# Lightweight convolution and MetaFormer block: the second group's x and tap products moved ahead, the third group's y stored by another queue

## The chip, the cores and the metric

The kernel runs on one core of a Trainium2 chip. The core has five engines that run side by side, each through its own queue in order: TensorE (PE in the profile, its weight loads PEld), VectorE (DVE), ScalarE (ACT), GpSimd (POOL) and SyncE (SP, which here only issues DMAs). The metric is the device time of one execution in microseconds (us); smaller is better. All data are float32.

## The reference

`x` has shape (8, 4224, 192), batch by sequence by channels. The first half is a causal depthwise convolution: 8 heads of 24 channels, 7 taps for each head, softmax over the taps. The second half is a layer norm without bias, two matrix products with a relu between them, and a residual:

```python
w = softmax(weight)                                   # 8 heads x 7 taps
y[b, s, h, :] = sum_k w[h, k] * x_padded[b, s + k, h, :]
xn = (y - mean(y)) / sqrt(var(y) + 1e-6) * g_ln
out = y + maximum(xn @ w_ch1, 0.0) @ w_ch2            # 192 -> 768 -> 192
```

## The kernel before, in words

**Groups.** The 8 x 4224 rows are laid on 128 partitions and cut into groups numbered from 0. Group 0 has 6 rows for each partition, group 1 the 8 rows for each partition that are left over at the ends of the batches, every later group 16 (the last one 10). In what follows x1, y1 and so on are the x and y of group 1; "the second group's x" is x1, "the third group's y" is y2, "the fifth x" is x4. y0 and y1 share one tile (rows 0 to 5 and 6 to 13), as do their later forms.

**The steps for one group.** `load_x` brings x with six rows of overlap. `first_tap` has ScalarE write y = tap 0 times x, head by head; `conv` has VectorE add the other taps into y, one instruction for each tap and head (L415). From group 2 on `second_tap` has ScalarE write the second tap's product into a tile of its own (`tb`), which four accumulating DMAs, issued by GpSimd in `add_in_parts` (L407), add into y; group 2's product lies in `room` and is added by VectorE (L1056). `transpose` turns y into blocks of 32 for TensorE (`yt`), `moments` takes the statistics, `root` has GpSimd compute the inverse deviation. TensorE multiplies by w1 (L521) and by w2 (L793, or L846); `store_y` writes y to the output, and the scaled result of the second product is later added there by accumulating DMAs (L942).

**Order.** The order is written out by hand: each engine does its instructions in the order in which the code issues them, and waits for the others by semaphores. Groups 0 and 1 go through plain products (`up`, `down`); from group 2 on `up_mixed` and `down_fast` make seven products instead of eight out of sums of quarters (`sums_of_quarters`, `sums_of_y`, on VectorE and GpSimd). Part of their sums are added by accumulating DMAs from GpSimd's queue (`close` with a part, L599, tiles `parts_cs` and `parts_tb`), part by VectorE straight from the accumulator banks (L641). Relus in place are ScalarE's L648.

**The banks.** The eight accumulator banks are taken in turn, singly (`take_bank`) or by four (`take_set`). A product that takes a set waits until ScalarE or VectorE has emptied it: in `up`, block f waits for the eviction (L511) of block f - 2, or for the copies of w1 if these took the set.

**The beginning.** The weights come as 64-bit words. `split_words`, `join_low`, `join_sign` and `join_product` make floats of them on VectorE and ScalarE; w1 in three parts s (x0 is on its way meanwhile), w2 after group 0's convolution. A load with `gate=True` is held until VectorE has written one element of its tile. `centre_w1` has TensorE take the mean out of w1 and do three of group 0's heads by `conv_on_pe`; `copies_of_w1` spreads w1 over four blocks of 32 partitions by TensorE, and ScalarE copies them out (L358). The third of these calls stands in `up`, behind block 1 of group 0.

**SyncE's queue** in this stretch: w1's words, x0, w2's words (L988, into `raw`), x1 (L140), y0's store, x2, y1's store, x3, x4 (L149, when x2's buffer is free), y3's store. y2's store (L487) is issued by GpSimd, inside `up_mixed(2)`.

Of the kernel before, what the change touches and what calls it, by code (L numbers as in the profile page):

```python
# [16 lines left out]
def kernel(  # L17
# [29 lines left out]
    nc = tc.nc  # L47
    PSUM = bass.MemoryType.PSUM
    B, S, D = x.shape
    H, K = weight.shape  # L50
# [41 lines left out]
    def rows_of_out(g, j1, j2):  # L92

        b, j0, n = groups[g]
        if b is not None:
            return [(slice(0, P), outr[b, :, (j0 + j1) * D : (j0 + j2) * D])]
        left = out[:, P * R : S].rearrange("b (p r) d -> p b (r d)", p=LP)
        return [(slice(0, P), left[:, :, j1 * D : j2 * D])]
# [17 lines left out]
    def take_bank():  # L116
        i = turn[0] % 8
        turn[0] = i + 1
        return all_banks[:, i]
# [126 lines left out]
    def join_low(raw, mant, power):  # L246
        mant = mant.bitcast(F32)
        nc.vector.scalar_tensor_tensor(
            out=mant, in0=raw[:, :, 0], scalar=2.0**-52, in1=mant, op0=ALU.mult, op1=ALU.add
        )  # L250
# [64 lines left out]
    def tap_matrices(h, ks=range(K)):  # L315
        for k in ks:
            nc.scalar.mul(diag[:, h - PE_HEADS[0], k, :], unit, taps[:, h, k : k + 1])

    def conv_on_pe(h):
        n = groups[0][2]  # L320
        cs = slice(h * GRP, h * GRP + GRP)
        pc = take_bank()[:, 0 : n * GRP]
        for k in range(K):
            nc.tensor.matmul(  # L324
                pc, diag[:, h - PE_HEADS[0], k, :], xg[0][:, k : k + n, cs],
                start=(k == 0), stop=(k == K - 1),
            )
        nc.scalar.copy(y[0][:, 0:n, cs], pc.rearrange("p (j d) -> p j d", d=GRP))

    def centre_w1():  # L330
        pm = [take_bank()[:, 0:FH] for r in range(2)]
        for r in range(2):
            nc.tensor.matmul(pm[r], share[0], w1f[:, r, :], start=True, stop=False)
        conv_on_pe(PE_HEADS[2])
        for r in range(2):
            nc.tensor.matmul(pm[r], share[1 + r], w1f[:, 2, :], start=False, stop=True)
        tap_matrices(PE_HEADS[1], range(3))
        for r in range(2):
            nc.scalar.copy(mean[:, FH * r : FH * r + FH], pm[r])
        tap_matrices(PE_HEADS[1], range(3, K))  # L340
        conv_on_pe(PE_HEADS[0])
        copies_of_w1(0, [(q, 0) for q in range(NQ)])
        conv_on_pe(PE_HEADS[1])
        copies_of_w1(2, [(NQ, 0), (NQ + 1, 0), (NQ, 1), (NQ + 1, 1)])

    def copies_of_w1(s, parts):
        pw = [take_bank() for q in range(NQ)]
        for q in range(NQ):
            rows = slice(C * q, C * q + C)
            nc.tensor.matmul(pw[q][:, 0:FH], copy[rows], w1f[rows, s, :], start=True, stop=False)  # L350
        for q, (c, r) in enumerate(parts):
            rows = slice(C * q, C * q + C)
            nc.tensor.matmul(
                pw[q][:, 0:FH], less[rows], mean[rows, FH * r : FH * r + FH],
                start=False, stop=True,
            )
        for q, (c, r) in enumerate(parts):
            nc.scalar.copy(w1[:, c, FH * r : FH * r + FH], pw[q][:, 0:FH])  # L358
# [8 lines left out]
    def first_tap(g, heads=(0, H)):  # L367
        n = groups[g][2]
        if g == 1:

            y[g] = y[0][:, groups[0][2] :]
        elif heads[0] == 0:
            y[g] = ypool.tile([P, J, D], F32, tag="y", name=f"y{g}")
        for h in range(*heads):
            cs = slice(h * GRP, h * GRP + GRP)
            nc.scalar.mul(y[g][:, 0:n, cs], xg[g][:, 0:n, cs], taps[:, h, 0:1])  # L376
# [32 lines left out]
    def conv(g, k0=1, k1=K, heads=(0, H)):  # L409
        n = groups[g][2]  # L410
        t = xg[g]
        for k in range(k0, k1):
            for h in range(*heads):
                cs = slice(h * GRP, h * GRP + GRP)
                nc.vector.scalar_tensor_tensor(  # L415
                    out=y[g][:, 0:n, cs], in0=t[:, k : k + n, cs], scalar=taps[:, h, k : k + 1],
                    in1=y[g][:, 0:n, cs], op0=ALU.mult, op1=ALU.add,
                )
# [65 lines left out]
    def store_y(g, queue=nc.sync):  # L484
        n = groups[g][2]
        for ps, rows in rows_of_out(g, 0, n):
            queue.dma_start(out=rows, in_=y[g][ps, 0:n].rearrange("p j d -> p (j d)"))  # L487
# [54 lines left out]
    def up(g):  # L542


        n = groups[g][2]
        hidden_tile(g)
        for f in range(NF):
            banks = take_set()
            rows_of_tiles(banks, yt[g][:, 0:n], w1[:, :, f * P : f * P + P])
            evict_up(g, f, banks[:, :, 0 : n * C])  # L550
            if g == 0 and f == 0:
                first_tap(1, heads=(0, H // 2))
            elif g == 0 and f == 1:
                copies_of_w1(1, [(q, 1) for q in range(NQ)])
                scale_power(words_2[2])
            elif g == 0 and f < 4:
                first_tap(1, heads=(2 * f, 2 * f + 2))
            between(g, f)

# [41 lines left out]
    def up_mixed(g, ahead, pending):  # L601
# [71 lines left out]
        next(pending, None)  # L673
        p.product(Y, a22, p.t[2], False)
        p.close(p.c21, Y, two.c22[:, 0:1])
        if g == 2:
            store_y(g, nc.gpsimd)
        p.product(X, s4, p.b22, False)
        p.evict(X, p.c12, True)

# [300 lines left out]
    for s in range(3):  # L981
        if s:
            join_low(*words_1[s])
            join_sign(*words_1[s])
        join_product(w1f[:, s], *words_1[s], ga if s < 2 else gb)
        if s == 1:
            nc.vector.memset(raw2[0:1, 0:1, :], 0)
    nc.sync.dma_start(  # L988
        out=raw2.rearrange("p (c d) w -> p c (d w)", d=D),
        in_=w2_words.rearrange("(c p) d -> p c d", p=P),  # L990
    )
    load_x(1, gate=True)
    tap_matrices(PE_HEADS[0], range(4))
    first_tap(0, heads=(0, PE_HEADS[0]))
    tap_matrices(PE_HEADS[0], range(4, K))
# [20 lines left out]
    for g in range(NG):  # L1016
        last = g + 1 == NG
        if g + 2 < NG and g != 1:
            load_x(g + 2)
        if g < 2:  # L1020
            up(g)
            work = []
        else:
            work = (up_last if last else up_mixed)(g, ahead(g), pending)
            pending = iter(())
        if g == 0:
            early = CH * C // GRP
            join_low(*words_2)
            conv(1, 1, 5, heads=(0, early))
            join_sign(*words_2)  # L1030
            join_product(w2flat, *words_2)
            conv(1, 5, K, heads=(0, early))
            transpose(1, 0, CH)
            conv(1, heads=(early, H))
            first_tap(2)
            second_tap(2)
            let_in(w1sums[:, 1])
            sums_of_quarters(w1sums[:, 1], w12, w22)
            sums_of_quarters(w1sums[:, 0], w11, w1sums[:, 1])
            store_y(1)  # L1040
            load_x(3, later=True, gate=True)
            transpose(1, CH, NC)
            moments(0)
            moments(1)
            down(g)
            steps = root(0)
            next(steps)
            add_in_parts(2, tb[2], third[2])
            clear_pad(3)
            next(steps)  # L1050
            sums_of_quarters(w1sums[:, 2], w21, w1sums[:, 0])
            continue
        if g == 1:
            conv(2, 3)
            flat = [v.rearrange("p j d -> p (j d)") for v in (y[2], tb[2])]
            nc.vector.tensor_tensor(flat[0], *flat, op=ALU.add)  # L1056
            transpose(2)
            fourth_sum = sums_of_y(2, nc.gpsimd)
            nc.vector.tensor_tensor(w12, w12, w11, op=ALU.subtract)
            moments(2)  # L1060
            down(g)
            fourth_sum()
            sums_of_quarters(w2sums[:, 2], b12, b22)
            sums_of_quarters(w2sums[:, 0], b12, b11)
            sums_of_quarters(w2sums[:, 1], b22, w2sums[:, 0])
            sums_of_quarters(w2sums[:, 3], b21, w2sums[:, 1])
            continue
        if g + 3 < NG:
            store_y(g + 1)
        results = down_fast(g, work)  # L1070
        if last:
            finish_fast(g, 1, *results)
            for j in range(fast[g]):
                add(g, j, ots[g][:, j])
            store(g, 0, fast[g])
            for j in range(fast[g], groups[g][2]):
                rows = take_bank()[:, 0:D]
                down_row(rows, lambda f: rows_left[g][:, j - fast[g], f])
                add(g, j, rows)
                store(g, j, j + 1)  # L1080
        elif g % 2 == 0:
            pending = root(g)
# [30 lines left out]
```

## Time and profile before

| | |
|---|---|
| median of 3 runs | 948.33 us (947.61 to 949.34) |
| profiled execution | 948.87 us, of which 947.0 us are the span from the first instruction to the last |
| busy: TensorE | 939.2 us |
| busy: VectorE, ScalarE, GpSimd | 893.5, 716.4, 338.4 us |
| granted TensorE clock | 1.0 |
| groups 0 and 1 up to the first product of group 2 | 0 to 79.5 us of the span |
| group 2: products with w1, with w2 | 79.5 to 107.3, 107.3 to 135.8 us |

Times in the profile count from the start of the span and belong to one execution, the profiled one. A line of the timeline gives start, length, engine, source line, operation, output and inputs with shapes, and how many instructions are merged; brackets hold the time for which the engine was idle before it, and what ended that. A busy engine may still be one that waits for nothing but itself, so what matters is who is late when another engine stands still.

### The profile page before, as it was taken

The page shows a single profiled execution, that of the slowest core. Times are in us where ns is not written, and L with a number is a line of the kernel's source. Part 1 is how long each engine was busy: PE and PEld are TensorE (multiplying, and loading weights), DVE is VectorE, ACT ScalarE, POOL GpSimd, SP SyncE. Part 2 cuts the span into 40 slices and gives each one's busy share as a digit, 9 for nine tenths or more (in the row PEclk, how much of TensorE's full clock was granted, in tenths as well). Part 3 has the DMA queues.
Part 4 walks back from the last instruction along what each step waited for, and adds up shares of the span by engine and source line. Part 5 has one row for each costly group of instructions (what it writes and reads, how often), then busy time and mean ns, then how long its engine had stood idle before and what let it go on. Part 6 is the DMA issues. An engine that isn't in the chain of part 4 may idle for free.

```text
span 947.0 us, 38441 instructions
## 1 busy us (share of the span) xinstructions
PE 939.2 (99%) x17096; PEld 756.4 (80%) x17096; DVE 893.5 (94%) x1492; ACT 716.4 (76%) x1275; POOL 338.4 (36%) x448
## 2 busy tenths in 40 slices
PE   9999999999999999999999999999999999999998
PEld 7999779697889969687786968778796877869687
DVE  8998999999999999999999999999999999998896
ACT  7974877879687787959778795978879597877643
POOL 1097144321724136142443217231451424331130
PEclk9999999999999999999999999999999999999999
DMA  8288897988879797897979887897978979776611
GB/s 231 97 212 191 208 255 141 253 161 205 183 154 259 144 255 146 223 195 141 258 143 249 158 225 160 174 254 136 260 146 229 178 159 223 136 110 114 113 53 61
DMA packets 37851, 170.37 MB, mean 180 GB/s; under 512 B 4149, under 2 KB 5430, under 8 KB 31671
## 3 DMA queue, kind: packets, MB, share of 16 engines
q0 software_dynamic: 30672, 104.61, 59.6%
q1 hardware_dynamic: 7008, 63.31, 18.3%
q8 instruction: 134, 2.20, 0.9%
q14 instruction: 31, 0.25, 0.1%
q10 hardware_dynamic: 6, 0.00, 0.0%
HBM read 38.93 MB, written 49.35 MB: 93 GB/s over the span
## 4 chain that ended last, share of the span: by engine, by line
PE 88%; POOL 5%; DMA 3%; DVE 2%; ACT 1%; issue 1%; POOLq 0%; ACTq 0%
PE ps L846 45%; PE ps L521 41%; DVE y L415 2%; DMA room<-room 1%; POOL d L458 1%; DMA room<-parts_cs 1%; PE ps L363 1%; POOL w1sums L571 1%; PE ps L324 1%; POOL d L476 1%; PE ps L793 0%; POOL room L407 0%; POOL room L599 0%; POOL ysums L595 0%; ACT room L635 0%
## 5 line engine op out<-in xcount | busy, mean ns | idle before, releaser
L415 DVE SCALAR_TENSOR_TENSOR y<-xg,taps,y 128x384 f32<-128x384 f32 (+3 forms) x710 | 357.2, 580 | 4.0 <-ACT room L635 3.5
L846 PE MATMUL ps<-room,w2sums 128*32 128x256 f32 (+1 forms) x4464 | 244.4, 376 | 0.5 <-issue 0.5
L635 ACT COPY room<-ps 128x512 f32<-128x512 f32 (+1 forms) x225 | 180.6, 844 | 63.2 <-PE ps L521 62.6
L521 PE MATMUL ps<-yt,w 32*128 32x256 f32 (+3 forms) x4092 | 225.8, 365 | 0.3 <-ACT room L511 0.3
L846 PEld LDWEIGHTS ps<-room,w2sums 128*32 128x32 f32 x4464 | 154.1, 110 | 84.7 <-issue 1.6
L521 PEld LDWEIGHTS ps<-yt,w 32*128 32x128 f32 x4092 | 203.7, 185 | 17.2 <-issue 6.8
L846 PE MATMUL ps<-room,w 128*32 128x256 f32 (+1 forms) x3456 | 191.8, 373 | 0.3 <-DVE room L641 0.2
L889 DVE TENSOR_TENSOR room<-room 128x1024 f32<-128x1024 f32 x135 | 154.6, 1221 | 18.1 <-PE ps L846 14.2
L846 PEld LDWEIGHTS ps<-room,w 128*32 128x32 f32 x3456 | 116.1, 110 | 67.1 <-DVE room L641 5.2
L521 PE MATMUL ps<-ysums,w1sums 32*128 32x256 f32 (+1 forms) x2304 | 132.2, 371 | 0.0
L521 PEld LDWEIGHTS ps<-ysums,w1sums 32*128 32x128 f32 x2304 | 121.5, 185 | 5.1 <-issue 0.2
L942 POOL DMA_DIRECT2D out_dram<-ot x59 | 51.0, 864 | 175.6 <-ACT ot L931 172.5
L852 ACT COPY cs<-ps 128x256 f32<-128x256 f32 (+1 forms) x192 | 70.9, 370 | 44.9 <-PE ps L846 44.5
L931 ACT ACTIVATE ot<-ot,r 128x192 f32<-128x192 f32 x238 | 101.0, 469 | 0.0
L648 ACT ACTIVATE room<-room 128x1024 f32<-128x1024 f32 x90 | 94.8, 1064 | 5.4 <-DMA room<-parts_cs 5.4
L407 POOL DMA_DIRECT2D y<-tb x59 | 52.2, 1382 | 112.1 <-ACT room L852 105.2
L376 ACT ACTIVATE y<-xg,taps 128x384 f32<-128x384 f32 (+3 forms) x141 | 72.8, 609 | 1.1 <-DMA xg<-in_x_dram 0.6
L521 PE MATMUL ps<-yt,w1sums 32*128 32x256 f32 (+1 forms) x1152 | 71.8, 371 | 0.1
L521 PE MATMUL ps<-ysums,w 32*128 32x256 f32 (+1 forms) x1152 | 71.2, 369 | 0.0
L446 DVE BATCH_NORM_STATS2 st<-y 128x6 f32<-128x192 f32 x264 | 70.2, 344 | 0.0
L852 ACT COPY room<-ps 128x256 f32<-128x256 f32 (+1 forms) x96 | 35.6, 370 | 40.9 <-PE ps L846 40.2
L384 ACT ACTIVATE tb<-xg,taps 128x384 f32<-128x384 f32 (+1 forms) x120 | 65.6, 626 | 0.0
(121 smaller groups left out, 966.6 us busy)
## 6 DMA issues: line engine op xcount, KB each, us to landing
xg<-in_x_dram SPq DMA_DIRECT2D x15, 2112.0 KB, 16.0
room<-room POOLq DMA_DIRECT2D x45, 512.0 KB, 5.1
y<-tb POOLq DMA_DIRECT2D x58, 384.0 KB, 8.5
out_dram<-ot POOLq DMA_DIRECT2D x57, 384.0 KB, 9.6
out_dram<-y SPq DMA_DIRECT2D x13, 1536.0 KB, 9.2
room<-parts_cs POOLq DMA_DIRECT2D x30, 512.0 KB, 6.9
room<-parts_tb POOLq DMA_DIRECT2D x15, 1024.0 KB, 7.6
out_dram<-y SPq DMA_DIRECT2D x2, 768.0 KB, 4.4
```

Of the source, the lines that this page charges most:

```text
L376: nc.scalar.mul(y[g][:, 0:n, cs], xg[g][:, 0:n, cs], taps[:, h, 0:1])
L384: nc.scalar.mul(dst[:, 0:n, cs], xg[g][:, k : k + n, cs], taps[:, h, k : k + 1])
L407: nc.gpsimd.dma_start(out=ends[0], in_=ends[1], accum_op=ALU.add)
L415: nc.vector.scalar_tensor_tensor(out=y[g][:, 0:n, cs], in0=t[:, k : k + n, cs], scalar=taps[:, h, k : k + 1], in1=y[g][:, 0:n, cs], op0=AL ...
L446: nc.vector.bn_stats(out=sums[g][:, j, :], in_=y[g][:, j, :])
L521: nc.tensor.matmul(banks[:, q, i * w + j1 * t : i * w + j2 * t], right[rows, c, P * i : P * i + P], left[rows, j1:j2, c, :], start=start, ...
L635: nc.scalar.activation(to, of, AF.Relu) if relu else nc.scalar.copy(to, of)
L648: nc.scalar.activation(c, c, AF.Relu)
L846: nc.tensor.matmul(dst[C * q : C * q + C, 0:w], right[:, f, C * c : C * c + C], left[:, f, q], start=(first and f == PAIR), stop=(f == PAI ...
L852: nc.scalar.copy(to[:, c], dst[:, 0:w].rearrange("p (j t) -> p j t", t=t))
L889: nc.vector.tensor_tensor(dst[:, f], left[:, f], right_of[:, f], op=op)
L931: nc.scalar.mul(ots[g][:, j, :], ots[g][:, j, :], rstd[g][:, j : j + 1])
```

## The change

Four things move; no arithmetic is added or taken away.

1. x1's load, with its gate, is issued behind the first part of w1 (s = 0), so it stands ahead of w2's words in SyncE's queue.
2. ScalarE's first-tap products of group 1: heads 0 and 1 go ahead of the first copies of w1, heads 2 and 3 ahead of the second; before, all four stood behind block 0 of group 0's up-projection.
3. On VectorE the second tap of group 1's heads 0 to 3 goes ahead of the first step of w2's join.
4. y2's store goes from GpSimd's queue to SyncE's, behind x4's load.

```diff
         tap_matrices(PE_HEADS[1], range(3, K))
         conv_on_pe(PE_HEADS[0])
+        first_tap(1, heads=(0, H // 4))
         copies_of_w1(0, [(q, 0) for q in range(NQ)])
         conv_on_pe(PE_HEADS[1])
+        first_tap(1, heads=(H // 4, H // 2))
         copies_of_w1(2, [(NQ, 0), (NQ + 1, 0), (NQ, 1), (NQ + 1, 1)])
...
             evict_up(g, f, banks[:, :, 0 : n * C])
-            if g == 0 and f == 0:
-                first_tap(1, heads=(0, H // 2))
-            elif g == 0 and f == 1:
+            if g == 0 and f == 1:
                 copies_of_w1(1, [(q, 1) for q in range(NQ)])
                 scale_power(words_2[2])
-            elif g == 0 and f < 4:
+            elif g == 0 and 2 <= f < 4:
                 first_tap(1, heads=(2 * f, 2 * f + 2))
...
         p.close(p.c21, Y, two.c22[:, 0:1])
-        if g == 2:
-            store_y(g, nc.gpsimd)
         p.product(X, s4, p.b22, False)
...
         join_product(w1f[:, s], *words_1[s], ga if s < 2 else gb)
-        if s == 1:
+        if s == 0:
+            load_x(1, gate=True)
+        elif s == 1:
             nc.vector.memset(raw2[0:1, 0:1, :], 0)
     nc.sync.dma_start(
         out=raw2.rearrange("p (c d) w -> p c (d w)", d=D),
         in_=w2_words.rearrange("(c p) d -> p c d", p=P),
     )
-    load_x(1, gate=True)
...
         if g + 2 < NG and g != 1:
             load_x(g + 2)
+        if g == 2:
+            store_y(g)
...
             early = CH * C // GRP
+            conv(1, 1, 2, heads=(0, early))
             join_low(*words_2)
-            conv(1, 1, 5, heads=(0, early))
+            conv(1, 2, 5, heads=(0, early))
             join_sign(*words_2)
```

## The prediction, made before the changed kernel was run

> **What bounds the kernel now.** I read the page first (busy shares, chain of waits), then the timeline of the first 140 us, because all edits act before the fourth group, then the stretches and the DMA issues around the moved transfers.
>
> The page: the first line is busy time and share by engine, the second the chain that ended last.
>
> ```profile
> PE 939.2 (99%) x17096; PEld 756.4 (80%) x17096; DVE 893.5 (94%) x1492; ACT 716.4 (76%) x1275; POOL 338.4 (36%) x448
> PE 88%; POOL 5%; DMA 3%; DVE 2%; ACT 1%; issue 1%; POOLq 0%; ACTq 0%
> ```
>
> TensorE (PE) has 947.0 - 939.2 = 7.8 us without work, start and end included. The change takes no matmul away, so it can only win where PE waits, and lose where it makes PE wait. The timeline (start, length, engine, line; in brackets the idle time before and what ended it) shows the first such place:
>
> ```profile
> 19.11 1.63 ACT L358 COPY w<-ps 128x384 f32<-128x384 f32 x4 [1.20 <-PE ps L353]
> 22.52 1.63 ACT L358 COPY w<-ps 128x384 f32<-128x384 f32 x4 [1.21 <-PE ps L353]
> 25.24 1.36 DVE L248 SCALAR_TENSOR_TENSOR spare<-raw,spare 128x1152 f32<-128x1152 uint32 x1 [0.58 <-ACT spare L232]
> 25.76 1.51 ACT L376 ACTIVATE y<-xg,taps 128x192 f32<-128x192 f32 x4
> 26.23 0.83 PE L350 MATMUL ps<-room 32*128 32x384 f32 x8
> 27.15 0.82 ACT L511 ACTIVATE room<-ps 128x768 f32<-128x768 f32 x1
> 28.02 8.08 PE L521 MATMUL ps<-yt,w 32*128 32x192 f32 x192 [0.32 <-ACT room L511]
> ```
>
> ScalarE (ACT) idles 1.20 and 1.21 us ahead of two copies of w1, then computes four tap products (1.51 us) ahead of the eviction at 27.15, for whose banks PE stands until 28.02. VectorE (DVE) idles 0.58 us ahead of w2's join. The second place, 80 us later:
>
> ```profile
> 76.64 3.54 POOL L407 DMA_DIRECT2D y<-tb  x4
> 87.45 14.91 DVE L415 SCALAR_TENSOR_TENSOR y<-xg,taps,y 128x384 f32<-128x384 f32 x28 [3.49 <-ACT room L635]
> 89.49 0.87 POOL L487 DMA_DIRECT2D out_dram<-y  x1
> 95.57 1.77 POOL L599 DMA_DIRECT2D room<-parts_cs  x2 [5.20 <-ACT parts_cs L635]
> 105.00 2.29 DVE L641 TENSOR_TENSOR room<-room,ps 128x2048 f32<-128x2048 f32 x1
> 107.34 4.42 PE L846 MATMUL ps<-room,w 128*32 128x256 f32 x72 [0.17 <-DVE room L641]
> 107.38 1.06 ACT L648 ACTIVATE room<-room 128x1024 f32<-128x1024 f32 x1 [1.26 <-DMA room<-parts_cs]
> 113.95 6.42 PE L846 MATMUL ps<-room,w2sums 128*32 128x256 f32 x113 [0.47 <-issue]
> ```
>
> DVE's 3.49 us are put down to ACT, but the semaphores end with the landing of the four adds into y3 (last one at 87.07). From 87.45 DVE works without a break to the sum that lets PE start at 107.34, so **y3's adds set PE's start there**. At 108.50 PE stands 0.27 us more, for the relu behind the landing of parts_cs (107.36). The gap at 113.95 is no stall: it is exactly 4.00 row steps of 0.2155 us, so records are missing.
>
> Which DMAs run meanwhile (stretch, busy time by engine, clock, mean busy share of the 16 DMA engines, GB/s), and two groups of issues with their time to landing:
>
> ```profile
> 76.00:78.00 2.00, 2.00 (x14) 2.00 (x14) 1.97 (x2) 0.17 (x1) 2.00 (x4) 1.00 0.00 0
> 78.00:80.00 2.00, 2.00 (x22) 1.77 (x24) 2.00 (x5) 0.41 (x1) 2.00 (x4) 1.00 1.10 195
> 96.00:102.00 6.00, 6.00 (x116) 5.74 (x112) 6.00 (x13) 4.77 (x4) 1.28 (x2) 1.00 1.03 334
> y<-tb POOLq DMA_DIRECT2D x4, 384.0 KB, 6.5
> out_dram<-y POOLq DMA_DIRECT2D x1, 1536.0 KB, 12.6
> ```
>
> The engines are idle from 76 to 78, then full with y3's adds.
>
> **x1 ahead of w2's words.** The gate now stands behind the first w1 product, which DVE ends at 9.10, so SyncE (SP) issues x1 at about 9.2 instead of 12.34. In the packet records SP's queue works in order: w2's packets run from 11.82 to 15.80, x1's from 15.29 to 22.38, landing 0.9 us later; x0's last packet ends at 10.97. So x1 starts between 10.3 and 11.0, needs the same 7.1 us, and lands at 18.3 to 18.9. w2's words follow: both together take 10.56 us, ending near 21.2, and w2's landing lagged its last packet by 1.2 us: 22.0 to 22.7, against DVE's first use at 22.46. I take a loss of 0.10 us on DVE (0 to 0.25). Queued behind w2 on SP, y0's store (21.34) waits for DVE anyway: nothing.
>
> **Two tap products ahead of each of two copies of w1.** Two products take 0.7 us (1.51 for four). ACT is free at 17.9 but now waits there for x1, with the copies, the next eviction of y0 and PE's first up-projection queued behind it. Landing at 18.3 to 18.9 ends the products at 19.0 to 19.6, against the copies' 19.11; 0.30 us of idle at 21.04 takes up the rest. The second pair fits into the 1.21 us. Cost nothing while x1 lands before about 19.3; if later, DVE and PE lose one for one.
>
> **The eviction at 27.15.** With the products gone it follows PE's end of that block (26.45), is done at 27.3, and PE goes on at 27.52, straight after the mean's matmuls: 0.50 us, and 0.11 us of slow start behind it, together -0.61 us. The copies of w1 move to 27.7 and end at 29.4, the next block that reads them begins at 29.5, so that gain holds by 0.1 us.
>
> **Four taps ahead of w2's join.** DVE fills its 0.58 us with them and is 0.58 - 0.10 = 0.48 us earlier from there. w2 is ready at 34.0 and PE needs it at 35.4. GpSimd (POOL) starts its sums on DVE's word (40.53 us idle ends at 46.22), so its chain up to y3's adds moves along: 76.64 becomes 76.16.
>
> **y2's store.** It leaves POOL's queue, where 0.87 us of issue lay before 5.20 us of idle time: nothing. On SP it stands behind x4's load and waits for the sum that ends y2 at 71.98 (71.5 after); SP has nothing else until 114.54. Its 128 packets of 0.485 us need 3.9 us of all 16 engines. In before they ran from 96.46 to 101.74, ahead of parts_cs. With them gone parts_cs lands some 3.9 us earlier, and PE's 0.27 us at 108.50 go.
> In the new place x4's packets end at 75.71 - 0.48 = 75.2, the store's at about 79.1, and y3's adds start at 78.08 - 0.48 = 77.6. So 1.5 us of store is left on the slowest engine, and the adds already fill the engines (share 1.10). Their delay c lies between 0 (engines that end x4 first have ended the store too) and 3.9 us (the whole store in the way). I take 1.2, near the 1.5 of the slowest engine, since the adds' semaphore needs all 16.
> The Trainium skill's opening page (Trainium Kernel Development and Optimization, Key Constraints) says that DMAs of SP, ACT and POOL share the same 16 engines and another queue only saves issue time; by that rule alone this edit is worth 0, against +0.93 (c less 0.27) by the rows. No run here moves a transfer's queue without its time.
>
> **Sum.** y3's adds land 1.2 - 0.48 = 0.72 us later than before, DVE's sum ends 0.72 later, and PE starts at 108.06, where it could have gone on at 106.6: the 0.61 us are given back there. Then -0.27. Net +0.45 us. The profiled execution took 948.87 (span 947.0, 1.87 around it), so 949.3; it lies 0.54 above the median of the runs, 948.33, so the forecast is **948.8**.
>
> **Rivals.**
> *No collision* (c = 0): PE starts the down-projection 0.48 earlier and saves 0.27: 948.33 - 0.75 = 947.6. For it: the engines' idle 76 to 78, and most of the store fits in. Against: 3.9 us do not fit between 75.2 and 77.6.
> *The store goes wholly ahead of the adds* (slower): c = 3.9, so 3.9 - 0.48 - 0.27 = +3.15: 951.5. The change loses from c = 0.75, and by 0.2% from c = 2.65. It needs the store to start only when the adds do. For it: x4's first packets were slow (issue 68.45, only 13 begun by 70.0), so its queue can slip. Against: x4 had ended 2.4 us before the adds. The Trainium skill's page DMA: Bandwidth & Descriptors (Queues, rings and completion order) has each engine take turns between its queues, by which the adds would wait at most for what is left of the store; no row of before has these two together.
> *x1 lands late*: if it needs its former 10.9 us from issue it lands at 20.1, and DVE and PE lose 0.8 of what they gained: 949.6. Against: 3.5 us of the 10.9 were w2's packets.
> *The change does not bite*: if the eviction at 27.15 still came late, the end would not move, since that gain is given back at 107 anyway.
>
> **How the numbers follow.** Forecast 0.5, no collision 0.25, store ahead 0.1, x1 late 0.1, rest 0.05. What a measurement can tell from no change is about 0.2%, 1.9 us. PE's waits that can go sum to 0.61 + 0.17 + 0.27 = 1.05 us, so faster by over 0.2% needs scatter: 0.05. Slower takes most of the store-ahead case and the bad end of late x1: 0.13. Same: 0.82. The range goes from the no-collision case less 0.4 of the runs' scatter (947.61 to 949.34), 947.2, to 950.8, which leaves out the worse half of store-ahead.
>
> **What would show it.** Right: PE's 0.32 at 28.02 gone; x1's products on ACT near 18.5; DVE's idle ahead of its 28 taps about 4.7 instead of 3.49, with their start near 88.2; PE's wait for the sum at L641 over 1 us, and none at parts_cs. Wrong: ACT waiting past 19.5 for x1, DVE's w2 split after 23, or the 28 taps starting before 87.0 or after 90.

## The result, and the profile after

The changed kernel is slower: 951.8 us in the median of 20 runs (950.35 to 955.10) against 949.0 for the kernel before (947.25 to 951.27), a ratio of 1.0035 with a 95% interval of 1.0028 to 1.0042. The forecast was 948.8, its range ended at 950.8. The profiled execution took 951.14 us, 949.3 of them the span: 2.3 us more than before.

Of the page, the busy times by engine, the chain of waits by engine, and one of the costliest groups (busy and mean ns of one; then the idle time ahead and what ended it):

```profile
PE 939.2 (99%) x17096; PEld 750.3 (79%) x17096; DVE 893.3 (94%) x1492; ACT 716.9 (76%) x1275; POOL 338.0 (36%) x447
...
PE 86%; POOL 1%; DMA 1%; DVE 0%; ACT 0%; issue 0%; ACTq 0%; POOLq 0%
...
L844 PE MATMUL ps<-room,w 128*32 128x256 f32 (+1 forms) x3456 | 192.8, 375 | 2.4 <-DVE room L641 2.4
```

The work of the engines is what it was. New is one wait: PE stood 2.4 us for DVE's sum at L641. The timeline at the first place (L378 is L376 of before, L513 is L511, L523 is L521):

```profile
19.04 0.80 ACT L378 ACTIVATE y<-xg,taps 128x192 f32<-128x192 f32 x2 [1.01 <-DMA xg<-in_x_dram]
26.49 0.81 ACT L513 ACTIVATE room<-ps 128x768 f32<-128x768 f32 x1 [0.60 <-PE ps L523]
27.52 8.01 PE L523 MATMUL ps<-yt,w 32*128 32x192 f32 x192
```

x1 is later than forecast (ACT waits 1.01 us for it), but in time for PE, whose first up-projection starts at 22.32 as before (22.33); the eviction stands at 26.49 instead of 27.15, and PE goes on at 27.52 without the 0.32 us of idle time, as forecast. Group 2 begins 0.58 us earlier on PE (78.90 instead of 79.48). The second place (L409 is L407, L417 is L415, L844 is L846):

```profile
76.33 3.54 POOL L409 DMA_DIRECT2D y<-tb  x4
89.08 14.90 DVE L417 SCALAR_TENSOR_TENSOR y<-xg,taps,y 128x384 f32<-128x384 f32 x28 [5.43 <-DMA y<-tb]
94.99 1.77 POOL L599 DMA_DIRECT2D room<-parts_cs  x2 [5.54 <-ACT parts_cs L635]
106.63 2.28 DVE L641 TENSOR_TENSOR room<-room,ps 128x2048 f32<-128x2048 f32 x1
108.96 5.78 PE L844 MATMUL ps<-room,w 128*32 128x256 f32 x72 [2.37 <-DVE room L641]
114.56 7.96 PE L844 MATMUL ps<-room,w2sums 128*32 128x256 f32 x144
122.33 4.07 PE L844 MATMUL ps<-room,w 128*32 128x256 f32 x72
```

GpSimd issued y3's adds 0.31 us earlier than before, yet they landed 1.62 us later (the last at 88.69 instead of 87.07). DVE's 28 taps start at 89.08 instead of 87.45, L641 follows at 106.63 instead of 105.00, and PE's down-projection at 108.96 instead of 107.34. And its first product, which no longer waits for a relu inside, still lasts longer: the next one follows after 5.60 us instead of 4.24. The start of that next one, in the kernel before:

```profile
111.58 1.90 PE L846 MATMUL ps<-room,w2sums 128*32 128x256 f32 x31
```

Why is in the stretches: busy time by engine, then the granted clock, the DMA share and GB/s. First the changed kernel, then the last stretch of the kernel before.

```profile
76.00:78.00 2.00, 2.00 (x15) 2.00 (x13) 1.97 (x2) 0.00 (x0) 2.00 (x4) 1.00 0.96 402
78.00:80.00 2.00, 2.00 (x30) 1.75 (x33) 2.00 (x6) 0.48 (x1) 2.00 (x4) 1.00 0.98 378
...
108.00:110.00 2.00, 1.04 (x20) 0.68 (x24) 1.90 (x2) 0.51 (x1) 0.00 (x0) 0.99 0.98 201
110.00:114.00 4.00, 4.00 (x52) 2.09 (x44) 4.00 (x8) 2.60 (x6) 0.00 (x0) 0.58 0.01 0
```

```profile
110.00:114.00 4.00, 3.53 (x67) 1.77 (x63) 4.00 (x9) 4.00 (x12) 0.64 (x1) 1.00 0.22 45
```

From 76 to 78 the DMA engines, empty before, are full with y2's store; 402 and 378 GB/s are its rate, where y3's adds alone ran at 195. And from 110 to 114 the granted TensorE clock averages 0.58, in the kernel before 1.00: the clock records show 0.5 from 109.98 to 113.39, **3.41 us at half clock**, beginning 1.02 us after PE went on. In that time a row step takes 0.427 us instead of 0.2155; eight such steps lost 1.69 us.

The two traces so add up: PE's start +1.62, half clock +1.69, the relu's wait -0.27, and -0.65 for a wait of PE at 113.95 that the trace of before has and this one has not: +2.39, against +2.30 at the third product (122.33 after 120.03) and +2.3 in the span.

### The profile page after: what moved, and what is told of

It reads as the page before. It is cut to its first block, busy times and chain, and to the rows that moved or that the text cites. A ratio compares the mean times of both kernels' runs of the same rounds, so it can differ in the third digit from the quotient of the medians.

```text
span 949.3 us, 38444 instructions
## 1 busy us (share of the span) xinstructions
PE 939.2 (99%) x17096; PEld 750.3 (79%) x17096; DVE 893.3 (94%) x1492; ACT 716.9 (76%) x1275; POOL 338.0 (36%) x447
## 4 chain that ended last, share of the span: by engine, by line
PE 86%; POOL 1%; DMA 1%; DVE 0%; ACT 0%; issue 0%; ACTq 0%; POOLq 0%
PE ps L844 45%; PE ps L523 41%; DMA room<-room 1%; PE ps L791 0%; ACT room L635 0%; DVE room L641 0%; POOL room L599 0%; POOL d L460 0%; POOL r L483 0%; POOL d L478 0%; POOL d L479 0%; DVE y L417 0%; DVE y L944 0%; POOL d L466 0%; POOL v L471 0%
## 5 line engine op out<-in xcount | busy, mean ns | idle before, releaser
L417 DVE SCALAR_TENSOR_TENSOR y<-xg,taps,y 128x384 f32<-128x384 f32 (+3 forms) x710 | 357.1, 578 | 6.0 <-DMA y<-tb 5.4
L844 PE MATMUL ps<-room,w2sums 128*32 128x256 f32 (+1 forms) x4464 | 243.6, 376 | 0.0
L523 PE MATMUL ps<-yt,w 32*128 32x256 f32 (+3 forms) x4092 | 225.6, 365 | 0.0
L844 PEld LDWEIGHTS ps<-room,w2sums 128*32 128x32 f32 x4464 | 150.7, 110 | 87.0 <-issue 0.3
L523 PEld LDWEIGHTS ps<-yt,w 32*128 32x128 f32 x4092 | 203.7, 185 | 16.5 <-issue 6.8
L844 PE MATMUL ps<-room,w 128*32 128x256 f32 (+1 forms) x3456 | 192.8, 375 | 2.4 <-DVE room L641 2.4
L887 DVE TENSOR_TENSOR room<-room 128x1024 f32<-128x1024 f32 x135 | 154.6, 1220 | 18.5 <-PE ps L844 15.8
L844 PEld LDWEIGHTS ps<-room,w 128*32 128x32 f32 x3456 | 114.5, 111 | 72.0 <-DVE room L641 7.4
L523 PE MATMUL ps<-ysums,w1sums 32*128 32x256 f32 (+1 forms) x2304 | 132.2, 371 | 0.0
L523 PEld LDWEIGHTS ps<-ysums,w1sums 32*128 32x128 f32 x2304 | 121.6, 185 | 5.0 <-issue 0.2
L409 POOL DMA_DIRECT2D y<-tb x59 | 52.1, 1361 | 110.9 <-ACT room L850 103.7
L378 ACT ACTIVATE y<-xg,taps 128x384 f32<-128x384 f32 (+3 forms) x141 | 72.8, 607 | 2.8 <-DMA xg<-in_x_dram 1.8
L523 PE MATMUL ps<-yt,w1sums 32*128 32x256 f32 (+1 forms) x1152 | 71.7, 372 | 0.1
L523 PE MATMUL ps<-ysums,w 32*128 32x256 f32 (+1 forms) x1152 | 71.2, 370 | 0.0
```

Of the source, the lines that this page charges most:

```text
L409: nc.gpsimd.dma_start(out=ends[0], in_=ends[1], accum_op=ALU.add)
L417: nc.vector.scalar_tensor_tensor(out=y[g][:, 0:n, cs], in0=t[:, k : k + n, cs], scalar=taps[:, h, k : k + 1], in1=y[g][:, 0:n, cs], op0=AL ...
L523: nc.tensor.matmul(banks[:, q, i * w + j1 * t : i * w + j2 * t], right[rows, c, P * i : P * i + P], left[rows, j1:j2, c, :], start=start, ...
L844: nc.tensor.matmul(dst[C * q : C * q + C, 0:w], right[:, f, C * c : C * c + C], left[:, f, q], start=(first and f == PAIR), stop=(f == PAI ...
L887: nc.vector.tensor_tensor(dst[:, f], left[:, f], right_of[:, f], op=op)
```

## The experiments

Theory A: the store stands ahead of y3's adds, so DVE's sum at L641 is late, PE is idle too long, and the clock drops. Theory B: edits 1 to 3 (x1 ahead of w2) lose time at the beginning. e1 to e4 were timed together on one chip, e5 to e8 on another and e9 and e10 on a third, each set against runs of the kernel before that were made with it. Diffs are against the changed kernel unless another is named.

### The four edits apart

**e1: edits 1 to 3, y2's store left with GpSimd.**

```diff
-        if g == 2:
-            store_y(g)
...
         p.close(p.c21, Y, two.c22[:, 0:1])
+        if g == 2:
+            store_y(g, nc.gpsimd)
```

> The first three edits, with y2's store left on GpSimd's queue as before. Theory A (the store on SyncE's queue is ahead of y3's adds in the 16 DMA engines, VectorE is late by that, TensorE stands 2.4 us and then runs 3.4 us at half clock): without the store there y3's adds land about 0.3 us earlier than before (near 86.8), TensorE starts the down-projection of group 2 near 107.0 with a gap under 0.5 us and no half clock; 0.3 to 0.6 us faster than before, ratio 0.9994 to 0.9997. Theory B (the loss comes from x1 ahead of w2 and the taps ahead of the copies, by way of the later VectorE and ScalarE work): still 1 us or more slower than before, ratio 1.001 or more.

Measured: 948.80 us against 948.68, ratio 1.0001 (0.9992 to 1.0009). The adds land at 87.06 and PE starts the down-projection at 107.32, both as before and not 0.3 us earlier, as theory A had expected; the clock stays at 1.0.

**e2: the kernel before with edit 4 alone** (diff against that).

```diff
+        if g == 2:
+            store_y(g)
...
-        if g == 2:
-            store_y(g, nc.gpsimd)
```

> The fourth edit alone: y2's store on SyncE behind x4, everything else as before. Theory A: y3's adds land 1.5 to 2.0 us later than before (88.6 to 89.1), TensorE's gap ahead of the down-projection is 1.7 to 2.2 us; 1.4 to 1.9 us of loss without a drop of the clock, 3.3 to 3.8 us with one (ratio 1.0015 to 1.004). Theory B: no slower than before, ratio 1.000 or less.

Measured: 952.62 us, ratio 1.0044 (1.0030 to 1.0058). So the loss is edit 4's and theory B falls; edits 1 to 3 neither lose nor win anything that these runs can tell. What they save at 28 us ends at PE's wait at 107, whose end the adds' landing sets. The ten runs come in steps, by the mean clock that each run records: one half-clock stretch of 3.41 us lowers that mean by 3.41 x 0.5 / 949 = 0.0018.

| mean granted clock | runs of e2, us |
|---|---|
| 0.999 | 948.82, 949.22 |
| 0.998 | 951.50, 952.15, 952.41, 952.84 |
| 0.995 to 0.997 | 954.21, 954.55, 954.99, 955.48 |

The profiled run is one of the first two. Its adds land at 88.47 and PE waits 1.64 us for L641 (at least 88.6 and 1.7 were expected), but its clock does not drop. In those two runs the late landing costs 0.3 us (949.0 against 948.7), less than the 1.4 to 1.9 expected without a drop; two runs are few. What lies above comes with a lower clock. The mean is a rough sign, though: every trace has a drop at the end too, of which 0 to 2.03 us lie in the span and take up to 0.0011 off the mean, and single runs do not fit: one of e4 shows 0.997 and took 948.78.

### The store elsewhere, and not at all

**e3: edits 1 to 3, the store on SyncE but held until DVE has done L641**, by one element of y2 copied onto itself.

```diff
-        if g == 2:
-            store_y(g)
...
         lower_sum(g, range(PAIR))
+        if g == 2:
+            touch = y[g][0:1, 0:1, 0:1]
+            nc.vector.tensor_copy(touch, touch)
+            store_y(g)
```

> The first three edits, and y2's store on SyncE held back until VectorE has made TensorE's last sum for group 2 (it copies one element of y2 onto itself there, and the store waits for that), so its packets run at about 110 to 114 us. Theory A: neither y3's adds nor the parts_cs adds meet the store; y3's adds land near 86.8, TensorE starts near 107.0, without the 0.27 us at the relu behind parts_cs; 0.6 to 1.2 us faster than before, ratio 0.9987 to 0.9994. Theory B: 1 us or more slower than before.

**e4: edits 1 to 3, y2's store left out.**

```diff
-        if g == 2:
-            store_y(g)
```

> The first three edits, and y2 is not stored at all (the output lacks it in the rows of group 2). This bounds what any place of the store can bring. Theory A: as the late store within 0.3 us, 0.6 to 1.2 us faster than before. Theory B: 1 us or more slower than before.

Measured: e3 947.79 us, ratio 0.9993 (0.9984 to 1.0002); e4 948.78, 0.9996 (0.9988 to 1.0005). Both are free of the loss and of the half clock; e3's adds land at 87.07 and PE waits 0.53 us for L641. It is not SyncE's queue that costs, but the store's 3.9 us of all 16 engines in this place. e3 is the fastest version measured, and still within what can be told from no change. e4's profile began late (x0 landed at 13.08 instead of 12.16), so its adds land at 87.89. It was expected to lie within 0.3 us of e3 and is 1.0 slower in the median, though the two intervals overlap.

### VectorE late without any transfer

In these the kernel before is kept, and DVE repeats 4, 8 or 6 statistics of y2 ahead of the last sum, 0.26 us each, the same input into the same output (diff against the kernel before, for eight).

```diff
+        if g == 2:
+            for j in range(8):
+                nc.vector.bn_stats(out=sums[g][:, j, :], in_=y[g][:, j, :])
         p.close(p.c21, X)
```

> The kernel before, with four statistics instructions of y2 repeated on VectorE (some 0.26 us each, so 1.04 us of VectorE time; same inputs, same result) just before the sum that closes y2. No transfer is changed. Theory A (the changed kernel loses because VectorE's sum at L641 comes late, TensorE idles over 2 us ahead of the down-projection, and its granted clock is then at half for some 3.4 us): the 28 taps wait for y3's adds 1.0 us less long than they did, 2.5 us in place of 3.49, or, since those adds follow y2's sum through GpSimd's steps, all of that moves by 1.04 us; either way TensorE idles at most some 1.2 us ahead of the down-projection, the clock stays at 1.0, and the time is 0 to 1.0 us over the kernel before. Theory R (the clock drop does not come from TensorE's idle time but from the store's traffic beside the adds): the same here. If the clock drops in this one, the bound of theory A is lower than it says.

> As the one with four repeated statistics instructions, but eight of them: some 2.08 us of VectorE time, no transfer changed. Theory A: if the delay reaches L641 in full, TensorE idles about 2.2 us ahead of the down-projection, the granted clock is then at half for some 3.4 us, and the time is 2.0 + 1.7 = 3.7 us over the kernel before. Theory R (the clock drop needs the store's traffic): TensorE idles 2.2 us, the clock stays at 1.0, and the time is 2.0 us over.

> The kernel before with six repeated statistics instructions of y2 on VectorE ahead of y2's last sum, between the ones with four and with eight; no transfer changed. Theory A (TensorE's idle time alone decides over the clock): the sum at L641 comes some 1.5 us later than in the kernel before, TensorE idles 1.5 to 2.1 us ahead of the down-projection; runs with up to 1.64 us have kept the clock at 1.0 and runs with 2.37 and more lost 3.4 us at half, so this one lies in the gap between: with the clock at 1.0 the time is 1.5 us over the kernel before, with the drop 3.2. Theory R (a longer VectorE chain costs its own length and no more): 1.5 us over and no drop, whatever the idle time.

Measured: with four 948.57 us, ratio 0.9999 (0.9991 to 1.0008); with six 951.49, 1.0022 (1.0014 to 1.0031); with eight 951.87, 1.0034 (1.0022 to 1.0047). Eight repetitions are 2.08 us of DVE and cost 3.21. The timeline of that one, and its stretches:

```profile
107.78 2.27 DVE L641 TENSOR_TENSOR room<-room,ps 128x2048 f32<-128x2048 f32 x1
110.10 5.71 PE L849 MATMUL ps<-room,w 128*32 128x256 f32 x72 [2.52 <-DVE room L641]
```

```profile
108.00:110.00 2.00, 0.00 (x0) 0.00 (x0) 2.00 (x1) 2.00 (x2) 0.00 (x0) 1.00 0.98 201
110.00:114.00 4.00, 3.90 (x44) 1.91 (x48) 3.90 (x6) 1.61 (x3) 0.00 (x0) 0.57 0.36 74
```

y2's store and y3's adds are where the kernel before has them (within 0.7 us), and yet PE, after 2.52 us of idle time, gets a mean clock of 0.57 from 110 to 114, as in the changed kernel: **the clock drop needs PE's idle time, and not the store's traffic in the new place**. That refutes theory R, by which the drop needs the store's traffic. Six repetitions give 2.06 us of idle time in the profiled run and the drop too; of their twelve runs nine show a mean clock of 0.998 and three 1.0. The one with four did not test what it was meant to: in its profile GpSimd's chain went through 6 us early (see the end), and PE's 1.48 us of idle time (at most some 1.2 were expected) left the clock alone.

### The adds ahead

If the landing of y3's adds is the cause, they might be issued earlier. In e7 and e8 GpSimd issues them ahead of the second half of `root` and of the third row of w1's sums; e7 has e3's late store, e8 the changed kernel's. e9 is e7 with x4's load behind the adds, its diff below against e7.

```diff
             clear_pad(3)
-            next(steps)
-            sums_of_quarters(w1sums[:, 2], w21, w1sums[:, 0])
             continue
         if g == 1:
+            next(steps)
+            sums_of_quarters(w1sums[:, 2], w21, w1sums[:, 0])
```

> Edits 1 to 3 of the change, y2's store on SyncE held back until after the sum at L641, and y3's four adds issued by GpSimd right after group 1's up-projection, ahead of its second half of the column sums and the third row of sums of w1. Theory A (the landing of y3's adds sets the start of the down-projection): the adds are issued some 6 us earlier, near 70.5, share the engines with x4 and land near 80; VectorE's idle of 3.49 us ahead of the 28 taps goes, TensorE's wait at L641 (0.5 in the kernel with the late store alone) goes, and so does what the earlier edits save; what GpSimd does after the adds comes no later. Time 946.5 to 948, 0.7 to 2 us below the kernel before. Theory R2 (VectorE has no slack behind the taps, or the sums of w1 come late instead): TensorE waits elsewhere before 120 and the time is that of the kernel before.

> The changed kernel (y2's store on SyncE behind the fifth x), with y3's adds issued some 6 us earlier, as in the one with the adds first. Theory A (the store on SyncE costs only because the adds stand behind it and VectorE's sum at L641 behind them): with the adds ahead of the store, they land before 83, VectorE does not wait for them, TensorE does not idle over 0.6 us ahead of the down-projection, the clock stays at 1.0, and the 2.8 us that the change lost are gone: 946.5 to 948.5. Theory R (the store costs wherever it meets other transfers of that stretch, or the third row of sums comes late): TensorE still waits 1 us or more for L641 and the time is 950 or more.

```diff
-        if g + 2 < NG and g != 1:
+        if g + 2 < NG and g not in (1, 2):
             load_x(g + 2)
...
             nc.vector.tensor_tensor(w12, w12, w11, op=ALU.subtract)
+            load_x(4, gate=True)
             moments(2)
```

> The one with the adds first (y3's adds issued near 71, y2's store behind L641), with x4's load moved behind them: its gate is a one-element write that VectorE does after the difference w12 - w11, near 78.3, so x4 is issued near 78.4 in place of 68.2. In the one with the adds first the adds moved only when x4's packets had left, and landed from 80.6 to 86.2. Theory A (on the way to VectorE's taps the transfers stand in one row, and what SyncE was given first goes first): without x4 ahead of them the adds land from 74.5 to 80, VectorE's idle ahead of the 28 taps (4.00 in the one with the adds first) goes, L641 is no longer late and TensorE's wait there is under 0.2; as TensorE only has some 0.3 to 0.5 us to win there, the time is 0.3 to 1.0 below the kernel before, within what five rounds can hardly tell from nothing. Theory R (the adds are slow by themselves, 1.9 us each, and only start when GpSimd's issue of 3.5 us and a latency of some 5 us are over): they land from 78 on, as late as 86 for the last, and VectorE still idles some 4 us.

Measured: e7 948.32 us, ratio 0.9998 (0.9990 to 1.0007); e8 949.20, 1.0003 (0.9994 to 1.0012); e9 949.39, 1.0006 (0.9998 to 1.0015). e7's expectation by theory A fell: issued at 71.05, 5.6 us ahead of before, its adds landed from 80.59 to 86.19, hardly earlier. PE's wait at L641 is gone, but PE stands 0.68 us for GpSimd's sums at 83.70 instead, as theory R2 had it. In the packet records only 9 of their packets began before 76, while x4's ran; x4 had been given out first, at 68.17. In e8 they share the engines with the store after x4 (from 76 to 81, 113 of the adds' packets begin and 112 of the store's) and land from 82.16 to 88.09, not before 83, so neither of its theories has all its numbers; that its PE waits only 1.00 us comes from PE being later itself. e9 shows that x4 held them (timeline):

```profile
70.75 3.50 POOL L409 DMA_DIRECT2D y<-tb  x4 [10.79 <-ACT tb L386]
82.62 19.65 DVE L417 SCALAR_TENSOR_TENSOR y<-xg,taps,y 128x384 f32<-128x384 f32 x28
83.89 1.58 PE L523 MATMUL ps<-ysums,w1sums 32*128 32x256 f32 x24 [0.49 <-POOL ysums L595]
103.45 2.87 PE L523 MATMUL ps<-yt,w1sums 32*128 32x256 f32 x48 [0.96 <-ACT room L635]
108.85 4.09 PE L848 MATMUL ps<-room,w 128*32 128x256 f32 x72
```

Without x4 ahead the same adds land from 75.72 to 81.31, and DVE starts its taps without a wait, as theory A said. But nothing is won: the 28 taps now take 19.65 us instead of 14.9 (the six that run beside GpSimd's sums, until 90.5, take 1.32 us each, the others 0.53 as before), GpSimd's sums come late for PE (0.49 us), PE waits 0.96 for a set of banks, and the down-projection starts at 108.85. The wait was not removed but handed on.

### The changed kernel twice more

The clock records of all profiles have one thing in common: between any two changes lie whole multiples of 3.413 us (30.0 of them from the first full clock to the drop; 273.0, 274.0 or 275.0 up to the end of the span where there is no drop). So the clock is set in steps of a grid, whose place differs from run to run.

> The changed kernel itself once more, for the place of its clock changes. In every profile so far the granted clock changed only on a grid of 3.413 us whose phase differs from run to run (between the changes lie 30.0 and 274.0 steps). Theory W (the clock is set for one step of that grid by TensorE's idle time within the step before): with the sum at L641 late by some 2.4 us, half clock follows if about 1.85 us or more of the idle time lie in one step (2.06 in one step gave it, 1.64 did not), and not if the step's edge cuts the idle time into parts that are both shorter; 951 with the drop, about 949.5 without, and near 954 if a second step falls to half elsewhere. Theory A0 (an idle time of over 2 us gives the drop wherever the edge lies): half clock in any case.

> The changed kernel a third time, with the same expectations as the repetition ahead of it: by theory W the drop hangs on whether 1.85 us or more of TensorE's idle time ahead of the down-projection lie in one step of the 3.413 us grid, by theory A0 it comes in any case.

Measured: 948.98 us without a drop, and 950.27 with one, beside 948.02 for the kernel before. The timeline of the first:

```profile
106.39 2.28 DVE L641 TENSOR_TENSOR room<-room,ps 128x2048 f32<-128x2048 f32 x1
108.73 3.61 PEld L844 LDWEIGHTS ps<-room,w 128*32 128x32 f32 x72 [2.23 <-DVE room L641]
108.73 4.09 PE L844 MATMUL ps<-room,w 128*32 128x256 f32 x72 [1.83 <-DVE room L641]
```

Its clock steps meet at 107.29, inside the 1.83 us of idle time, and the product takes its normal 4.09 us. The lines of three others on either side of the limit, e2, e10 and e12 (an undisturbed product takes 4.09 us):

```profile
108.74 4.09 PE L844 MATMUL ps<-room,w 128*32 128x256 f32 x72 [1.64 <-DVE room L641]
108.47 5.78 PE L849 MATMUL ps<-room,w 128*32 128x256 f32 x72 [2.06 <-DVE room L641]
108.55 5.59 PE L844 MATMUL ps<-room,w 128*32 128x256 f32 x72 [2.24 <-DVE room L641]
```

All profiles with a wait of 1 us or more at this place, with the longest part of it in one step of the grid:

| kernel | idle, us | in one step | clock after |
|---|---|---|---|
| e8 | 1.00 | 1.00 | 1.0 |
| e5 | 1.48 | 0.94 | 1.0 |
| e2 | 1.64 | 1.64 | 1.0 |
| changed, e11 | 1.83 | 1.44 | 1.0 |
| e10 | 2.06 | 2.06 | 0.5 for 3.41 us |
| changed, e12 | 2.24 | 1.92 | 0.5 for 3.41 us |
| changed, first | 2.37 | 2.37 | 0.5 for 3.41 us |
| e6 | 2.52 | 2.43 | 0.5 for 3.41 us |

The limit lies between 1.64 and 1.92 us in one step, or, if steps do not matter, between 1.83 and 2.06 in all. The table does not tell these two apart: e11, meant to, had under 2 us of idle time in all. For the steps speaks that one run of e6 kept a mean clock of 1.0 and took 950.70, 2.04 over the kernel before: just its delay, without the drop. Its idle time was not profiled.

## Why the prediction was wrong

**The first place: right for PE.** x1 came later than forecast: its products start at 19.04 (forecast near 18.5) and end at 19.84 (forecast 19.0 to 19.6). That cost PE nothing; the stall at 28 is gone, PE goes on at 27.52 exactly. DVE came out worse: w2's split started at 22.78, 0.32 later than before, where 0.10 was taken and 0.25 the worst, and its chain was 0.32 and not 0.48 earlier. Most of that is not the edit: x0 landed at 12.37 instead of 12.16 in this profile, DVE's first tap began at 12.95 instead of 12.68, and DVE did not wait for w2's words. In e11 and e12 the split starts at 22.41 and 22.45, as before; in e1, e3, e4, e7, e8 and e9 DVE waits 0.16 to 0.47 us for those words.

**The term c, mis-sized.** "I take 1.2, near the 1.5 of the slowest engine." It was 1.93: from the adds' issue to their last landing 12.36 us instead of 10.43 (and 12.52, 12.28 in the two repetitions). The last of x4's packets ended at 77.14, not 75.2, and the last of the store's at 80.80, not 79.1. By the issue the adds' first packet was due at 77.77; it came at 79.4, and until 80 only 22 of their 512 began. From 78 to 80 the store's 56 packets ran beside them, so the adds did not share with it here, they stood behind it. Part of the difference is x4: its 128 packets took 0.83 us each on average instead of 0.70, which makes 1.1 us on all 16 engines. They took 0.82 to 0.85 in all seven profiles in which another of these transfers was given out while x4 ran, 0.68 to 0.75 in the seven others; the prediction moved x4 as it was. Why they take longer is open.

The Trainium skill's page DMA: Bandwidth & Descriptors (Queues, rings and completion order) says that an engine takes a whole packet of some 9 to 17 descriptors from one queue before it turns to the next. The store's 128 packets of the records are 8 for each engine, if evenly spread; read as one such turn they would run as a block, which agrees with this trace but not with e8's. There the adds and the store both waited behind x4, and then began at the same rate, 113 and 112 packets in 5 us: sharing row by row, as the prediction had read "take turns". So the traces show both ways: a store already under way kept the adds out, two transfers that waited together shared. Whether the earlier start is what decides was not tested.

**The sign held, the way did not.** PE's start came 1.62 later where the sum had 0.72, the relu's wait of 0.27 went as forecast. That alone would have been +1.35, inside the range; e11, with 1.83 us of PE's idle time in place of 2.37 and without a drop, took 948.98 us, 0.96 over the run beside it. The base was off too: 948.33 was the median of three runs, twenty gave 949.0, which is 0.7 of the 3.0 us between forecast and result.

**The missing term.** No step of the sum asked what PE's clock does after a wait of over 2 us. "PE's wait for L641 sum over 1 us" stood in the text as a sign of being right; at 2.37 us it set off 3.41 us at half clock, 1.69 us. This pushed the result out of the range, and in 18 of 20 runs the mean clock was 0.998 or 0.996. (The other two, at 1.0 and 0.999, took 950.85 and 951.45, no less than the fastest at 0.998, 950.35; they were not profiled.) The Trainium skill's page TensorE: Matmul & The Clock Gate (Part 1) has a free-running window of 3413 ns, which agrees with the grid here, and a rule against idle gaps of over some 3.4 us. By that rule 2.37 us would be harmless; four profiles here dropped at 2.06 to 2.52.

**The rival that came close for another reason.** "The store goes wholly ahead" gave 951.5 with c = 3.9. The time was 951.8, with c = 1.93 and a clock drop: a number that fits is no proof of its mechanism.

**A misread line.** "The gap at 113.95 is no stall: records are missing." All 144 matmuls of that product are in the trace of before; the 0.65 us is a real wait, ended by "issue". It appears again in e1 (0.75 us by the same count, at 113.97) and in none of the other profiles. In both, a packet of an instruction queue ends just ahead of PE's restart (113.88 and 113.73), so a late instruction fetch may be it; but the other profiles have such a packet too, between 113.4 and 117.5, without a wait, and no run tested it.

**Still open.** Four runs of the changed kernel at a mean clock of 0.998 took 953.3 to 954.0, and e2's slowest four show 0.995 to 0.997; two of these (0.995, 0.996) are less than one half-clock step and the drop at the end leave. None of these was profiled, so where the further time goes is not known.

## What to carry to other kernels

A wait of TensorE has a price that jumps: up to 1.64 us it cost at most its length here, from about 2 us it cost 1.7 us more; so add up what an edit brings to a wait that already exists, and ask whether the total crosses that line. A transfer on an idle queue is not free: what counts is which transfers the same 16 engines get before the one that an engine waits for, and moving the late one's issue 5.6 us ahead (e7) brought its landing only 0.9 us ahead, while a larger one given out earlier (x4) still ran. When the landing of a transfer sets a start, compare issue-to-landing times of both traces; the issue alone moved 0.31 us the other way.

## What the runs showed of the hardware

- The granted TensorE clock changes only on a grid of 3.413 us with a phase of its own in each run; each drop ahead of the span's end lasted one step (four profiles). In e12 it began 0.32 us before PE went on, in the first profile of the changed kernel 1.02 us after.
- GpSimd's small steps can stand for long beside DVE's taps: an operation on 14 elements per partition, 0.43 to 0.45 us just before, took 8.65 us in the kernel before (at 59.81, until the taps ended) and 0.70 us in e5 (at 58.95), whose chain so came to the adds at 70.33 instead of 76.64. What decides between the two is open. In the other direction, six of e9's taps took 1.32 us each beside GpSimd's sums instead of 0.53.
- A store of 1536 KB ran at some 400 GB/s, the adds into y3 (384 KB each, 1.9 us apart) at about 200, with the 16 engines full in both. x4's packets took 0.70 us each in the kernel before and 0.83 with the store given out behind them.
